# Float64 weights made into fp32 words on the chip: the low word added as an integer

## The chip, the cores and the metric

One core of a Trainium2 chip runs the whole program. The time is device microseconds (us) of one execution. The names of the engines are those of the profile: PE is the matrix engine (TensorE), DVE is VectorE, ACT is ScalarE, POOL is GpSimd, and SP issues transfers.

## What is computed

Linear attention over 32 memory slots, then two MLPs. The weights `w_a`, `w_b`, `w_out` (of both MLPs) come as float64.

```
a = softmax(phi, axis=seq);  k_m = a^T k;  v_m = a^T v          # per batch (4) and head (8), seq 576
attn = softmax(q k_m^T / 8) v_m                                 # -> x: 2304 tokens x 512
x = ((x @ w_a) * (x @ w_b)) @ w_out                             # d_ff 1536
h = x @ w_in;  g = where(h > 0, h, exp(min(h, 0)) - 1)          # d_ff 2048
out = g @ w_out2                                                # 2304 x 512
```

## The kernel before

**Stages.** The attention runs first (L541 to L614), one batch after another: softmax of phi, key and value sums `pk`, scores `sc`, their softmax, and the transposed result `tp_x`, which `split_sb` (L76) splits into a high and a low fp32r part, `xhi` and `xlo`. From the last batch on the first MLP is woven in. `step_u` (L508) multiplies the weights by `v_m` (tile `u_ps`, result split into `u`), `steps_ab` (L616) makes the two products and multiplies them (`a_sb`, split into `gh`, `gl`), and `steps_o1` (L662) makes the product with `w_out` (`o1_ps`, which the profile shows as `o_ps`, evicted into `y`). The second MLP follows with `step_h` (L763, tile `h_ps`) and `steps_o2` (L802). Each product is three fp32r matmuls: high by high, high by low, low by high.

**Order.** Everything from the attention on stands in an order written out by hand, engine by engine. `step` (L253) issues the matmuls of one step on PE, then goes through a string of letters ("0f1a2"): `a` to `d` are the step's evictions, `f` is a share of the weight conversion, the digits are operations deferred by a step or two. Products lie in PSUM tiles `ps` of two banks, at first two of them, from the last batch on four. A matmul group that opens a tile waits until the tile's former content is read.

**Weights.** A unit is a block of weights of 128x512 float64 values; there are 68. A load puts it into one of three `raw` tiles. Then `piece` (L165) takes one slot of the unit at a time, seven slots for a unit. ACT makes `a`, the magnitude of the high word read as fp32 (`magnitude`, L118), and `lw`, the low word as a bf16 number (`low_word`, L126). DVE limits `a` (slot 0, L181), shifts it (slot 1, L184), splits off the low part of the unit before (slot 2, L163), puts the sign in (slot 3, L189), cuts the power of two out of `a` (slot 4, L193), scales `lw` by it (slot 5, L199), and adds (slot 6, L209). A unit of the stage "ab" is then ready as `ush`; others are split once more into a rounded high part (ACT, L154) and a rest (DVE, L163). With `ahead` set, ACT's two operations for the next unit are issued in slots 4 and 5, before the add. `fill(amount)` adds to a credit and runs one slot for each whole point of it; `fill(7)` in the attention runs one unit.

**Buffers.** `a` and `lw` have two tiles each, `a_sb` has three.

Of the kernel before, what the change touches and what calls it, by code (L numbers as in the profile page):

```python
# [7 lines left out]
F32 = mybir.dt.float32  # L8
F32R = mybir.dt.float32r
BF16 = mybir.dt.bfloat16  # L10
U32 = mybir.dt.uint32
U16 = mybir.dt.uint16
I64 = mybir.dt.int64
AF = mybir.ActivationFunctionType
ALU = mybir.AluOpType
AX = mybir.AxisListType
PSUM = bass.MemoryType.PSUM
LARGEST = float(0x1DFFFFF) * 2.0 ** 8


@with_exitstack
def attention_then_two_mlps(ctx, tc, q, kv, kv_left, phi, w_ab, w_o1, w_i2, w_o2, out):
# [13 lines left out]
    nc = tc.nc  # L36
    B, P, KC, S = q.shape
# [8 lines left out]
    HS = S // 2  # L46
# [15 lines left out]
    conv = ctx.enter_context(tc.tile_pool(name="conv", bufs=2, reuse_waits="tile"))  # L62
# [18 lines left out]
    NRAW, NSHORT, NPAIR, NLONG = 3,6,3,4  # L81
    units = []
# [19 lines left out]
    cu = {}  # L102
    seq = []
    ready = {}
    live = {False: 0, True: 0}
    state = {"loaded": 0, "n": 0, "slot": 0, "ahead": False}
# [11 lines left out]
    def magnitude(n):  # L118


        if n < NU and "a" not in cu[n]:
            a = conv.tile([P, 512], U32, tag="a", name="a", bufs=2)
            nc.scalar.activation(out=a.bitcast(F32), in_=cu[n]["h"].bitcast(F32), func=AF.Abs, scale=65536.0)  # L123
            cu[n]["a"] = a

    def low_word(n):  # L126
        if n < NU and "lw" not in cu[n]:
            t = conv.tile([P, 512], BF16, tag="lw", name="lw", bufs=2)
            nc.scalar.activation(out=t, in_=cu[n]["l"], func=AF.Copy, scale=2.0 ** -52)
            cu[n]["lw"] = t  # L130

    def ahead():
# [4 lines left out]
    def whole_words(n):  # L137
        return n < NU and units[n][0][0] == "ab"

    def to_hi(n):  # L140

        if n < 0 or whole_words(n):
            return True
        key, long, _ = units[n]
        if key == own:
            hi, lo = [pb.tile([P, 512], F32R, name=x, bufs=1) for x in ("ulh", "ull")]
        elif live[long] == (NLONG if long else NPAIR):
            return False
        else:
            live[long] += 1  # L150
            tag, nh, nl = ("ul", NLONG, NLONG) if long else ("us", NSHORT, NPAIR)
            hi = conv.tile([P, 512], F32R, tag=tag + "h", name=tag + "h", bufs=nh)
            lo = conv.tile([P, 512], F32R, tag=tag + "l", name=tag + "l", bufs=nl)
        nc.scalar.activation(out=hi, in_=cu[n]["a"].bitcast(F32), func=AF.Copy)  # L154
        ready[key] = hi, lo
        return True
# [8 lines left out]
    def piece():  # L165

        n, slot = state["n"], state["slot"]
        if n > NU:
            return False
        whole = n < NU  # L170
        if whole and slot == 0:
            magnitude(n)
            low_word(n)
        a = cu[n]["a"] if whole else None
        if slot == 1 and not to_hi(n - 1):
            return False
        if slot == 6 and whole_words(n) and live[False] == NSHORT:
            return False
        if whole and slot == 0:

            nc.vector.tensor_scalar(out=a.bitcast(F32), in0=a.bitcast(F32), scalar1=2.0, scalar2=LARGEST,  # L181
                                    op0=ALU.max, op1=ALU.min)
        elif whole and slot == 1:
            nc.vector.tensor_scalar(out=a, in0=a, scalar1=4, scalar2=1,  # L184
                                    op0=ALU.logical_shift_left, op1=ALU.logical_shift_right)
        elif slot == 2:
            to_lo(n - 1)
        elif whole and slot == 3:
            nc.vector.scalar_tensor_tensor(out=a, in0=cu[n]["h"], scalar=0x80000000, in1=a,  # L189
                                           op0=ALU.bitwise_and, op1=ALU.bitwise_or)  # L190
        elif whole and slot == 4:
            p2 = cu[n]["raw"].bitcast(BF16)[:, 0:512]
            nc.vector.tensor_scalar(out=p2.bitcast(U16), in0=a.bitcast(U16).rearrange("p (n w) -> p n w", w=2)[:, :, 1],  # L193
                                    scalar1=0xFF80, scalar2=None, op0=ALU.bitwise_and)
            cu[n]["p2"] = p2
            if state["ahead"]:
                low_word(n + 1)
        elif whole and slot == 5:
            nc.vector.tensor_tensor(out=cu[n]["lw"], in0=cu[n]["lw"], in1=cu[n]["p2"], op=ALU.mult)  # L199
            if ("unit",) not in seq:  # L200
                load_unit()
            if state["ahead"]:
                magnitude(n + 1)
        elif whole and slot == 6:
            to = a.bitcast(F32)
            if whole_words(n):
                live[False] += 1
                to = ready[units[n][0]] = conv.tile([P, 512], F32R, tag="ush", name="ush", bufs=NSHORT).bitcast(F32)
            nc.vector.tensor_tensor(out=to, in0=a.bitcast(F32), in1=cu[n]["lw"], op=ALU.add)  # L209
            if whole_words(n):  # L210
                cu.pop(n)
        slot += 1
        state["n"], state["slot"] = (n + 1, 0) if slot == 7 else (n, slot)
        return True

    def weights(key):
# [11 lines left out]
    credit = [0.0]  # L228

    def fill(amount):  # L230
        credit[0] += amount
        while credit[0] >= 1.0:
            credit[0] -= 1.0
            if not piece():
                credit[0] = 0.0


    RATE_AB, RATE_U, RATE_O1 = 1.0, 1.0, 3.0
    RATE_H, RATE_O2 = 2.5, 3.0
    ORDER, ORDER_H, ORDER_O2 = "0f1a2", "fab0c1df2", "0f1fa2"  # L240

# [38 lines left out]
    pu = es_u.enter_context(tc.tile_pool(name="pu", bufs=2, reuse_waits="tile"))  # L280
    rim = ctx.enter_context(tc.tile_pool(name="rim", bufs=1, side="right", reuse_waits="tile"))
    edge = rim.tile([P, 24], F32, name="edge")
    es_y = ExitStack()
    py = es_y.enter_context(tc.tile_pool(name="py", bufs=1, side="right", reuse_waits="tile"))
    y_all = py.tile([P, KC * NT], F32, name="y")
# [249 lines left out]
    es_b = ExitStack()  # L535
    with tc.manual_schedule():
        nc.gpsimd.memset(edge, 0.0)
        nc.scalar.activation(out=edge, in_=edge, func=AF.Exp)
        make_identity(nc, ident)
        nc.vector.tensor_reduce(out=parity, in_=ident.rearrange("p (s u) -> p u s", u=2), op=ALU.add, axis=AX.X)  # L540
# [24 lines left out]
        for i in range(B):  # L565
# [27 lines left out]
            else:  # L593
                es_l.close()
                es_p.close()
                pb = es_b.enter_context(tc.tile_pool(name="pb", bufs=2, side="right", reuse_waits="tile"))
# [18 lines left out]

        def steps_ab(f, b, amount):  # L616
            u = u_t.pop((f, b))
            a_sb = pb.tile([P, 2, HS], F32, tag="a_sb", name="a_sb", bufs=3)
            flat = a_sb.rearrange("p a s -> p (a s)")
            parts, done = [], 0  # L620
            while done < S:
                t = max(x for x in range(NB) if first[x] <= b * S + done)
                o = b * S + done - first[t]
                if o == 0:
                    if not inner:
                        inner.extend(pb.tile([P, N1], F32R, name=x, bufs=1) for x in ("gh", "gl"))
                    p = 256 * PLACE1[f % G][t]
                    g_t[f, t] = [x[:, p:p + BLOCKS[t]] for x in inner]
                w = min(S - done, BLOCKS[t] - o)
                parts.append((flat[:, done:done + w], *[x[:, o:o + w] for x in g_t[f, t]]))  # L630
                done += w
            for n in range(2):
                ps = pstile("ab_ps")

                def pe():
                    for kk in range(2):
                        for i, (w, x) in enumerate(((0, xhi), (0, xlo), (1, xhi))):
                            for h in range(2):
                                nc.tensor.matmul(  # L639
                                    ps[:, h, 0:HS], u[:, kk, w, n * P:n * P + P], x[b][:, kk, h * HS:(h + 1) * HS],  # L640
                                    start=(kk == 0 and i == 0), stop=(kk == 1 and i == 2),
                                )

                def evac():
                    if n == 0:
                        nc.scalar.activation(out=a_sb, in_=ps[:, :, 0:HS], func=AF.Copy)  # L646
                    else:
                        nc.vector.tensor_tensor(out=a_sb, in0=a_sb, in1=ps[:, :, 0:HS], op=ALU.mult)
                        defer(1, lambda: [nc.scalar.activation(out=gh, in_=a, func=AF.Copy) for a, gh, _ in parts])  # L649
                        defer(2, lambda: [nc.vector.tensor_tensor(out=gl, in0=a, in1=gh.bitcast(F32), op=ALU.subtract)  # L650
                                          for a, gh, gl in parts])

                step(pe, evac, amount)
# [59 lines left out]
        for kind, *args in order:  # L713
# [6 lines left out]
            else:  # L720
# [6 lines left out]
                t = b - 1  # L727
# [128 lines left out]
        for f in range(NF2):  # L856
            for k in range(NPART):
                t = TURN2[f % G][k] if f else k
# [63 lines left out]
```

## Time and profile before

| | us |
|---|---|
| median of 3 runs | 790.51 (789.45 to 790.68) |
| the profiled execution, its own time | 790.06 |
| its span, first to last instruction | 788.3 |
| PE busy in it | 768.9 (98%) |
| PE weight loads (PEld) | 675.4 (86%) |
| DVE busy | 594.8 (75%) |
| ACT busy | 408.9 (52%) |

The span is the time from the first to the last instruction; 1.8 us of the execution lie outside it. The rows further down come from this one execution. Matmuls are pipelined and their ends are modelled, so a stretch in which PE is shown busy can still hold waits; the starts of the matmuls tell it. The granted clock is 1.00 in every stretch up to the last matmul.

### The profile page before, as it was taken

The numbers are of one execution on the slowest core, as the hardware profiler recorded it, in microseconds if no ns is written. First come the engines' busy times: TensorE is split into PE (matmuls) and PEld (weight loads), VectorE is DVE, ScalarE is ACT, GpSimd is POOL, SyncE is SP. The second block draws the span as 40 slices with busy tenths as digits, with TensorE's granted clock in tenths as the row PEclk, the third lists the DMA queues.
The fourth block names the chain that finished last, engine by engine and source line by source line (L and its number), as shares of the span: only waits on it lengthen the run. The fifth ranks groups of instructions, "written<-read, shape, count | busy, mean of one in ns | idle before, by whom it ended". The sixth has DMA issues, their size and how long they took to land.

```text
span 788.3 us, 12416 instructions
## 1 busy us (share of the span) xinstructions
PE 768.9 (98%) x5084; PEld 675.4 (86%) x5084; DVE 594.8 (75%) x977; ACT 408.9 (52%) x684; POOL 38.8 (5%) x83
## 2 busy tenths in 40 slices
PE   4899999999999999999999999999999999999997
PEld 4788889888998999899888888888888888888886
DVE  5799985877877787787997438778877877885564
ACT  4555764534362435253688555556456625762460
POOL 2000000000000000000000000000000000000000
PEclk9999999999999999999999999999999999999999
DMA  9970232111212121122002001101111110100006
GB/s 340 409 281 27 58 104 72 57 61 54 81 29 81 55 81 55 54 68 68 27 5 87 17 1 53 54 28 54 54 36 46 54 54 27 53 1 1 1 1 241
DMA packets 17066, 57.70 MB, mean 73 GB/s; under 512 B 1776, under 2 KB 1776, under 8 KB 17008
## 3 DMA queue, kind: packets, MB, share of 16 engines
q0 software_dynamic: 8784, 31.99, 13.5%
q1 hardware_dynamic: 8224, 24.91, 8.2%
q8 instruction: 40, 0.66, 0.3%
q14 instruction: 18, 0.15, 0.1%
HBM read 52.17 MB, written 4.72 MB: 72 GB/s over the span
## 4 chain that ended last, share of the span: by engine, by line
PE 89%; DVE 5%; ACT 1%; issue 0%; DVEq 0%
PE h_ps L775 25%; PE o_ps L822 25%; PE ab_ps L639 18%; PE o_ps L675 18%; PE u_ps L522 2%; DVE ssm L485 1%; DVE y L490 1%; DVE u L533 0%; DVE y L474 0%; DVE xlo L78 0%; DVE smx L473 0%; DVE a L189 0%; ACT y L683 0%; ACT a L123 0%; PE tp_x L498 0%
## 5 line engine op out<-in xcount | busy, mean ns | idle before, releaser
L639 PE MATMUL ab_ps<-xhi,u 128*128 128x288 f32 x768 | 139.1, 298 | 0.1
L639 PEld LDWEIGHTS ab_ps<-xhi,u 128*128 128x128 f32 x768 | 114.5, 188 | 6.3 <-ACT gh L649 3.7
L822 PE MATMUL o_ps<-ull,g2h 128*128 128x512 f32 x288 | 112.1, 389 | 0.0
L822 PE MATMUL o_ps<-ulh,g2h 128*128 128x512 f32 x288 | 112.0, 389 | 0.0
L775 PE MATMUL h_ps<-yl,ush 128*128 128x512 f32 (+1 forms) x320 | 107.6, 369 | 0.0
L775 PE MATMUL h_ps<-yh,usl 128*128 128x512 f32 (+1 forms) x320 | 107.6, 368 | 0.0
L775 PE MATMUL h_ps<-yh,ush 128*128 128x512 f32 (+1 forms) x320 | 107.2, 367 | 0.0
L822 PE MATMUL o_ps<-ulh,g2l 128*128 128x512 f32 x288 | 100.3, 389 | 0.0
L794 DVE SCALAR_TENSOR_TENSOR e<-e,th 128x512 f32<-128x512 f32 (+1 forms) x64 | 48.3, 755 | 61.5 <-ACT e L791 61.1
L785 ACT ACTIVATE e<-h_ps 128x512 f32<-128x512 f32 (+1 forms) x64 | 41.6, 651 | 91.7 <-PE h_ps L775 85.6
L639 PE MATMUL ab_ps<-xlo,u 128*128 128x288 f32 x384 | 82.1, 295 | 0.0
L675 PE MATMUL o_ps<-gh,ulh 128*128 128x512 f32 (+1 forms) x240 | 72.9, 369 | 1.6 <-ACT y L683 1.6
L646 ACT ACTIVATE a_sb<-ab_ps 128x576 f32<-128x576 f32 x48 | 31.3, 653 | 80.9 <-PE ab_ps L639 80.9
L675 PE MATMUL o_ps<-gl,ulh 128*128 128x512 f32 (+1 forms) x240 | 72.7, 368 | 0.0
L675 PE MATMUL o_ps<-gh,ull 128*128 128x512 f32 (+1 forms) x240 | 72.6, 367 | 0.0
L797 DVE TENSOR_TENSOR g2l<-e,g2h 128x512 fp32r<-128x512 f32 (+1 forms) x64 | 48.4, 756 | 24.9 <-ACT g2h L796 24.5
L775 PEld LDWEIGHTS h_ps<-yh,ush 128*128 128x128 f32 x320 | 59.5, 188 | 8.5
L775 PEld LDWEIGHTS h_ps<-yh,usl 128*128 128x128 f32 x320 | 59.3, 188 | 7.5
L775 PEld LDWEIGHTS h_ps<-yl,ush 128*128 128x128 f32 x320 | 59.2, 188 | 7.3
L834 DVE TENSOR_TENSOR y<-o_ps,y 128x1024 f32<-128x1024 f32 (+1 forms) x44 | 51.0, 1194 | 18.0 <-PE o_ps L822 17.8
L822 PEld LDWEIGHTS o_ps<-ulh,g2l 128*128 128x128 f32 x288 | 54.0, 188 | 11.3
L822 PEld LDWEIGHTS o_ps<-ulh,g2h 128*128 128x128 f32 x288 | 54.1, 188 | 11.2
(95 smaller groups left out, 1273.6 us busy)
## 6 DMA issues: line engine op xcount, KB each, us to landing
raw<-in_w_o_dram POOLq DMA_DIRECT2D x27, 512.0 KB, 3.9
raw<-in_w_ab_dram POOLq DMA_DIRECT2D x18, 512.0 KB, 3.8
kv_t<-in_kv_dram SPq DMA_DIRECT2D x16, 512.0 KB, 9.9
raw<-in_w_i_dram POOLq DMA_DIRECT2D x16, 512.0 KB, 3.8
y<-in_q_dram SPq DMA_DIRECT2D x8, 576.0 KB, 10.3
out_dram<-y SPq DMA_DIRECT2D x8, 512.0 KB, 2.8
raw<-in_w_ab_dram SPq DMA_DIRECT2D x6, 512.0 KB, 9.1
phi_t<-in_phi_dram SPq DMA_DIRECT2D x3, 576.0 KB, 10.0
```

The source lines that it names most:

```text
L485: nc.vector.tensor_reduce(out=sm, in_=at, op=ALU.add, axis=AX.X)
L490: nc.vector.tensor_tensor(out=at, in0=at, in1=sm.to_broadcast(list(at.shape)), op=ALU.mult)
L522: nc.tensor.matmul(ps[j:j + M, o, k * 256:k * 256 + 256], vt[r, 2 * p + o, 2 * k + c], w[r, c * 256:c * 256 + 256], start=True, stop=True, ...
L639: nc.tensor.matmul(ps[:, h, 0:HS], u[:, kk, w, n * P:n * P + P], x[b][:, kk, h * HS:(h + 1) * HS], start=(kk == 0 and i == 0), stop=(kk == ...
L646: nc.scalar.activation(out=a_sb, in_=ps[:, :, 0:HS], func=AF.Copy)
L675: nc.tensor.matmul(ps[:, s], w[:, cc], g[:, s], start=(n == 0 and i == 0), stop=(n == len(fs) - 1 and i == 2),)
L775: nc.tensor.matmul(ps[:, s], w[:, c], x[:, c, s], start=(c == 0 and i == 0), stop=(c == KC - 1 and i == 2),)
L785: nc.scalar.activation(out=e, in_=ps, func=AF.Relu, scale=-1.0)
L794: nc.vector.scalar_tensor_tensor(out=e, in0=e, scalar=1.0, in1=th, op0=ALU.add, op1=ALU.mult)
L797: defer(1, lambda: nc.vector.tensor_tensor(out=gl, in0=e, in1=gh.bitcast(F32), op=ALU.subtract), 1)
L822: nc.tensor.matmul(ps[:, k, :], g[:, c * P:(c + 1) * P], w, start=(f == fs[0] and i == 0), stop=(f == fs[-1] and i == 2),)
L834: nc.vector.tensor_tensor(out=dst, in0=ps[:, 0:n], in1=dst, op=ALU.add)
```

## The change

The arithmetic of a unit is made in another way. ACT now writes `lw` in fp32: the low word times 2^-27 plus an offset of 2^25, which is a [128,1] tile `offset` (a POOL memset at the start). The offset fixes the exponent, so that the rounded low word stands as an integer in the float's bits. DVE shifts `a` left by three bits only, combines the sign with an exclusive or, and adds the bits of `lw` as a 32-bit integer. The slots of L193 and L199 are gone, and a unit has five slots. The built program makes the integer add with one instruction over 1024 16-bit halves in a row of 128 partitions; the order shows it as ISA. `low_word(n + 1)` is now issued behind slot 3 and `magnitude(n + 1)` behind the add; the next unit's load is issued behind slot 3. `fill` multiplies its amount by 5/7, the head's `fill(7)` is so one unit as before, and RATE_U goes from 1.0 to 1.4, which is one slot as before. `a_sb` has two tiles in place of three. The orders on PE and SP are the same as before; POOL has one memset more.

```diff
-LARGEST = float(0x1DFFFFF) * 2.0 ** 8
+LARGEST = float(0x1DFFFFF) * 2.0 ** -11
...
-            nc.scalar.activation(out=a.bitcast(F32), in_=cu[n]["h"].bitcast(F32), func=AF.Abs, scale=65536.0)
+            nc.scalar.activation(out=a.bitcast(F32), in_=cu[n]["h"].bitcast(F32), func=AF.Abs, scale=0.125)
...
-            t = conv.tile([P, 512], BF16, tag="lw", name="lw", bufs=2)
-            nc.scalar.activation(out=t, in_=cu[n]["l"], func=AF.Copy, scale=2.0 ** -52)
+            t = conv.tile([P, 512], U32, tag="lw", name="lw", bufs=2)
+            nc.scalar.activation(out=t.bitcast(F32), in_=cu[n]["l"], func=AF.Identity, scale=2.0 ** -27, bias=offset)
...
-        if slot == 6 and whole_words(n) and live[False] == NSHORT:
+        if slot == 4 and whole_words(n) and live[False] == NSHORT:
             return False
         if whole and slot == 0:
 
-            nc.vector.tensor_scalar(out=a.bitcast(F32), in0=a.bitcast(F32), scalar1=2.0, scalar2=LARGEST,
+            nc.vector.tensor_scalar(out=a.bitcast(F32), in0=a.bitcast(F32), scalar1=2.0 ** -18, scalar2=LARGEST,
                                     op0=ALU.max, op1=ALU.min)
         elif whole and slot == 1:
-            nc.vector.tensor_scalar(out=a, in0=a, scalar1=4, scalar2=1,
-                                    op0=ALU.logical_shift_left, op1=ALU.logical_shift_right)
+            nc.vector.tensor_scalar(out=a, in0=a, scalar1=3, scalar2=None, op0=ALU.logical_shift_left)
         elif slot == 2:
             to_lo(n - 1)
         elif whole and slot == 3:
             nc.vector.scalar_tensor_tensor(out=a, in0=cu[n]["h"], scalar=0x80000000, in1=a,
-                                           op0=ALU.bitwise_and, op1=ALU.bitwise_or)
-        elif whole and slot == 4:
-            p2 = cu[n]["raw"].bitcast(BF16)[:, 0:512]
-            nc.vector.tensor_scalar(out=p2.bitcast(U16), in0=a.bitcast(U16).rearrange("p (n w) -> p n w", w=2)[:, :, 1],
-                                    scalar1=0xFF80, scalar2=None, op0=ALU.bitwise_and)
-            cu[n]["p2"] = p2
-            if state["ahead"]:
-                low_word(n + 1)
-        elif whole and slot == 5:
-            nc.vector.tensor_tensor(out=cu[n]["lw"], in0=cu[n]["lw"], in1=cu[n]["p2"], op=ALU.mult)
+                                           op0=ALU.bitwise_and, op1=ALU.bitwise_xor)
             if ("unit",) not in seq:
                 load_unit()
             if state["ahead"]:
-                magnitude(n + 1)
-        elif whole and slot == 6:
-            to = a.bitcast(F32)
+                low_word(n + 1)
+        elif whole and slot == 4:
+            to = a
             if whole_words(n):
                 live[False] += 1
-                to = ready[units[n][0]] = conv.tile([P, 512], F32R, tag="ush", name="ush", bufs=NSHORT).bitcast(F32)
-            nc.vector.tensor_tensor(out=to, in0=a.bitcast(F32), in1=cu[n]["lw"], op=ALU.add)
+                ready[units[n][0]] = conv.tile([P, 512], F32R, tag="ush", name="ush", bufs=NSHORT).bitcast(F32)
+                to = ready[units[n][0]].bitcast(U32)
+            nc.vector.tensor_tensor(out=to, in0=a, in1=cu[n]["lw"], op=ALU.add)
             if whole_words(n):
                 cu.pop(n)
+            if state["ahead"]:
+                magnitude(n + 1)
         slot += 1
-        state["n"], state["slot"] = (n + 1, 0) if slot == 7 else (n, slot)
+        state["n"], state["slot"] = (n + 1, 0) if slot == 5 else (n, slot)
         return True
...
-        credit[0] += amount
+        credit[0] += amount * 5 / 7
...
-    RATE_AB, RATE_U, RATE_O1 = 1.0, 1.0, 3.0
+    RATE_AB, RATE_U, RATE_O1 = 1.0, 1.4, 3.0
...
+    offset = rim.tile([P, 1], F32, name="offset")
...
+        nc.gpsimd.memset(offset, 2.0 ** 25)
...
-            a_sb = pb.tile([P, 2, HS], F32, tag="a_sb", name="a_sb", bufs=3)
+            a_sb = pb.tile([P, 2, HS], F32, tag="a_sb", name="a_sb", bufs=2)
```

DVE in the attention of the second batch: one unit (L181 to L209, now L181 to L200) between the softmax of phi and that of the scores. Before:

```order
L181 TENSOR_SCALAR a<-a 128x512
L184 TENSOR_SCALAR a<-a 128x512
L189 SCALAR_TENSOR_TENSOR a<-raw,a 128x512
L193 TENSOR_SCALAR raw<-a 128x512
L199 TENSOR_TENSOR lw<-lw,raw 128x512
L209 TENSOR_TENSOR ush<-a,lw 128x512
L362 TENSOR_REDUCE nm<-phi_t 128x1 x2
L473 TENSOR_REDUCE smx<-sc 128x32
```

And now:

```order
L181 TENSOR_SCALAR a<-a 128x512
L184 TENSOR_SCALAR a<-a 128x512
L188 SCALAR_TENSOR_TENSOR a<-raw,a 128x512
L200 ISA ush<-a,lw 128x1024
L356 TENSOR_REDUCE nm<-phi_t 128x1 x2
L467 TENSOR_REDUCE smx<-sc 128x32
```

Two instructions of the six are gone, and nothing else has moved there.

DVE around the first `o1` products (`gl`: rest of `g`; `ull`: rest of a unit; `u`: rest of `u_ps`, which frees that PSUM tile). Just ahead of the first row stands that unit's L193. Before:

```order
L199 TENSOR_TENSOR lw_1175<-lw_1175,raw_608 128x512
L650 TENSOR_TENSOR gl_789<-a_sb_1143,gh_788 128x576
L209 TENSOR_TENSOR a_1191<-a_1191,lw_1175 128x512
L181 TENSOR_SCALAR a_1213<-a_1213 128x512
L184 TENSOR_SCALAR a_1213<-a_1213 128x512
L163 TENSOR_TENSOR ull_1227<-a_1191,ulh_1226 128x512
L189 SCALAR_TENSOR_TENSOR a_1213<-raw_914,a_1213 128x512
L193 TENSOR_SCALAR raw_914<-a_1213 128x512
L199 TENSOR_TENSOR lw_1208<-lw_1208,raw_914 128x512
L209 TENSOR_TENSOR ush_1248<-a_1213,lw_1208 128x512
L181 TENSOR_SCALAR a_1246<-a_1246 128x512
L533 TENSOR_TENSOR u_1250<-u_ps_1251,u_1250 128x4x256
```

And now:

```order
L200 ISA a_1181<-a_1181,lw_1166 128x1024
L645 TENSOR_TENSOR gl_783<-a_sb_1133,gh_782 128x576
L181 TENSOR_SCALAR a_1200<-a_1200 128x512
L184 TENSOR_SCALAR a_1200<-a_1200 128x512
L163 TENSOR_TENSOR ull_1213<-a_1181,ulh_1212 128x512
L188 SCALAR_TENSOR_TENSOR a_1200<-raw_904,a_1200 128x512
L200 ISA ush_1230<-a_1200,lw_1197 128x1024
L181 TENSOR_SCALAR a_1232<-a_1232 128x512
L527 TENSOR_TENSOR u_1234<-u_ps_1235,u_1234 128x4x256
```

The add of the first unit stands ahead of `gl` instead of behind it, and L193 and L199 of both units are gone ahead of the instruction that frees the PSUM tile.

ACT at the same place, from the two `u` evictions on. Before:

```order
L531 ACTIVATE u_1270<-u_ps_1271 128x4x256
L683 ACTIVATE y_77<-o1_ps_1291 128x512
L683 ACTIVATE y_77<-o1_ps_1301 128x512
L129 ACTIVATE lw_1310<-raw_1189 128x512
L123 ACTIVATE a_1315<-raw_1189 128x512
```

And now:

```order
L525 ACTIVATE u_1254<-u_ps_1255 128x4x256
L678 ACTIVATE y_78<-o1_ps_1275 128x512
L129 ACTIVATE lw_1286<-raw_1164,offset_74 128x512
L678 ACTIVATE y_78<-o1_ps_1289 128x512
L123 ACTIVATE a_1299<-raw_1164 128x512
```

A low word now stands between the evictions of the first two `o1` tiles. The PSUM tiles are dealt out otherwise, too: the third `o1` tile of this group took over the tile that the first eviction freed, and now takes the one that the rest of `u` (L533, now L527) frees.

## Rows read from the trace of the kernel before

**Rows 1.** Busy time by stretch: us, then PE, PEld, DVE, ACT, POOL; clock; DMA.

```profile
76.00:105.00 29.00, 27.43 (x244) 23.26 (x243) 27.27 (x51) 22.43 (x37) 2.23 (x4) 1.00 0.25 74
105.00:783.70 678.70, 678.70 (x4036) 598.04 (x4034) 506.51 (x807) 345.44 (x561) 31.32 (x56) 1.00 0.16 50
```

**Rows 2.** Chain of work that ended last: start, us, what.

```profile
130.01 9.59 PE ab_ps L639 x72
...
759.23 24.49 PE o_ps L822 x108
```

**Rows 3.** Groups of instructions by line and shape: busy us, mean ns, idle before.

```profile
L129 ACT ACTIVATE lw<-raw 128x512 bf16<-128x512 uint32 x68 | 44.9, 661 | 14.0 <-DVE ush L209 14.0
...
L199 DVE TENSOR_TENSOR lw<-lw,raw 128x512 bf16<-128x512 bf16 x68 | 28.7, 421 | 1.2
...
L479 ACT ACTIVATE y<-y 128x1024 f32<-128x1024 f32 x4 | 4.2, 1062 | 0.3 <-DVE y L474 0.3
...
L396 ACT ACTIVATE a_left<-tl_a,parity 128x128 f32<-128x128 f32 x8 | 2.5, 367 | 0.0
...
L438 ACT ACTIVATE vt<-pt 128x128 f32<-128x128 f32 x4 | 1.1, 283 | 0.0
```

**Rows 4.** Timeline, DVE, second batch: start us, us, instruction, idle before.

```profile
34.51 0.43 DVE L193 TENSOR_SCALAR raw<-a 128x512 uint16<-128x512 uint16 x1
...
35.43 0.69 DVE L209 TENSOR_TENSOR ush<-a,lw 128x512 f32<-128x512 f32 x1
...
41.15 1.22 DVE L78 TENSOR_TENSOR xlo<-tp_x,xhi 128x1024 fp32r<-128x1024 f32 x1
```

**Rows 5.** Timeline, PE, where the third batch's scores begin.

```profile
41.76 0.27 PE L388 MATMUL tl_a<-ident,rest 128*128 128x128 f32 x1
42.48 3.81 PE L447 MATMUL sc<-y 128*128 128x128 f32 x32 [0.45 <-issue]
```

**Rows 6.** Timeline, PE, the first ab product.

```profile
58.24 0.42 PE L639 MATMUL ab_ps<-xlo,u 128*128 128x288 f32 x2
58.74 0.80 PE L639 MATMUL ab_ps<-xhi,u 128*128 128x288 f32 x4
```

**Rows 7.** Timeline, DVE, softmax sums of the third batch.

```profile
53.88 1.53 DVE L485 TENSOR_REDUCE ssm<-y 128x32 f32<-128x1024 f32 x2
```

**Rows 8.** Timeline, ACT, the exponentials ahead of them.

```profile
52.49 1.36 ACT L479 ACTIVATE y<-y 128x1024 f32<-128x1024 f32 x2
```

**Rows 9.** Timeline, DVE, the second ab product.

```profile
67.71 0.75 DVE L648 TENSOR_TENSOR a_sb<-a_sb,ab_ps 128x576 f32<-128x576 f32 x1
```

**Rows 10.** Timeline, PE, that product and the last transposes.

```profile
66.78 0.42 PE L639 MATMUL ab_ps<-xhi,u 128*128 128x288 f32 x2
...
74.54 0.43 PE L639 MATMUL ab_ps<-xhi,u 128*128 128x288 f32 x2
75.41 1.06 PE L498 MATMUL tp_x<-ident,y 128*128 128x128 f32 x8 [0.43 <-DVE y L490]
```

**Rows 11.** Timeline, DVE, at the first o1 products.

```profile
95.59 0.43 DVE L193 TENSOR_SCALAR raw<-a 128x512 uint16<-128x512 uint16 x1
...
101.65 1.22 DVE L533 TENSOR_TENSOR u<-u_ps,u 128x1024 fp32r<-128x1024 f32 x1
```

**Rows 12.** Timeline, ACT, at the first o1 products.

```profile
97.78 0.63 ACT L154 ACTIVATE ulh<-a 128x512 fp32r<-128x512 f32 x1 [0.37 <-DVE a L209]
...
100.35 1.93 ACT L531 ACTIVATE u<-u_ps 128x1024 fp32r<-128x1024 f32 x2
```

**Rows 13.** Timeline, PE, the third o1 tile of the second group.

```profile
100.86 0.39 PE L675 MATMUL o_ps<-gh,ull 128*128 128x512 f32 x1
102.81 0.50 PE L675 MATMUL o_ps<-gh,ulh 128*128 128x512 f32 x1 [1.56 <-ACT y L683]
```

**Rows 14.** Waits: engine, line, waited for: us, times, longest.

```profile
DVE a L181 <- ACT a L123: 9.5, 8, 2.4
```

**Rows 15.** Windows of line L181 alone: DVE busy us and count.

```profile
76.00:105.00 29.00, 2.11 (x5) 1.00 0.25 74
```

## The prediction

> **What bounds the kernel now.** I read the busy time by stretch first, then the chain, then the timelines of the places where PE stands. From 105 us to 783.7 us PE is busy all of the time at full granted clock [rows 1], and in the chain its matmuls follow one another at 24.49/108 = 0.227 us for 512 columns and 9.59/72 = 0.133 us for 288 [rows 2]; so nothing waits in these 679 us. DVE has 506.5 of these 678.7 us to do, ACT 345.4 [rows 1]. A cheaper unit on DVE is worth nothing there. Up to 32 us the start waits for transfers that the change leaves alone. What DVE can give back lies between 32 and 105 us, in four waits of PE: 0.45 us before the third batch's scores [rows 5]; 58.74 - (58.24 + 0.27) = 0.23 us in the first ab product, a pair of whose matmuls takes 0.27 us otherwise [rows 2, 6]; 75.41 - (74.54 + 0.27) = 0.60 us before the last transposes [rows 10]; 102.81 - (100.86 + 0.23) = 1.72 us before the third o1 tile of the second group [rows 13]. Together 3.0 us: no more can be won.
>
> **The unit on DVE.** L193 and L199 leave. From the start of L193 to the start of the add it is 35.43 - 34.51 = 0.92 us [rows 4]; so much earlier the add can start. Its own price is not in the trace. It has 1024 halves for each partition. The nearest rows are a two-tensor instruction over 512 bf16 elements at 0.421 us, the old fp32 add over 512 at 0.69, and one over 1024 fp32 elements at 1.22 [rows 3, 4, 11]. At the rate of bf16 elements 1024 halves cost what 512 fp32 elements do, 0.69; at the rate of fp32 elements 1.22. I take 0.69, since halves are 16 bits wide as in the bf16 row, which is the row of its kind; 1.22 is the upper bound. [...]
>
> The trace shows the 16-bit row at 0.421 us beside 0.69 for as many fp32 elements [rows 3, 4]. [...]
>
> **The low word on ACT.** Same shape, fp32 out, and a [128,1] operand as bias, where there was an immediate. The trace has 0.661 us for the old form; for 128x128 an activation with a [128,1] operand takes 0.367 us and one without 0.283 [rows 3]. So the price of the operand is 0 to 0.09 us; I take 0.09. Over 68 units it is 6 us of an engine that has 22.4 of 29 us to do in its fullest stretch [rows 1], and counts only where ACT stands in the path, below.
>
> **Place 1, 42 us.** PE's score matmuls wait for the PSUM tile that L78 reads, from 41.15 to 42.37 [rows 4]; PE itself is ready at 41.76 + 0.27 = 42.03 [rows 5]. The unit at 34.51 is in front of L78 on DVE, and so L78 ends at 42.37 - 0.92 = 41.45. Next late is PE itself, the wait is gone: 0.45 us.
>
> **Place 2, 58 us.** DVE's chain to the rest of `u` goes through one more unit (0.92 us) and then through L485 at 53.88 [rows 7]. L485 needs the exponentials, the larger of which ends at 52.49 + 1.06 = 53.55 [rows 3, 8] and follows PE, now 0.45 us earlier: 53.1. So the chain moves by 0.78 us, PE by 0.45, and 0.33 is more than the 0.23 us of the wait: all of it goes.
>
> **Place 3, 75 us.** DVE's product starts at 67.71, and right ahead of it stands L193; it leaves, L189 goes behind the product, and the shorter L184 comes in its place. The product then starts when its matmuls are done, at 66.78 + 0.42 = 67.20 and a semaphore later, 0.45 us earlier instead of 0.51 [rows 9, 10]. From it the path goes over `gh`, a low word and `u` on ACT, then to the softmax that PE waits for. The low word costs its 0.09. Won: 0.36 of 0.60 us. What is late next is the same softmax.
>
> **Place 4, 101 us.** Today `ulh` waits on ACT for DVE's add, 0.37 us, and starts at 97.78 [rows 12]. The new add starts at 95.59 [rows 11] and ends at 96.28; `ulh` is then held by ACT alone, which is free at 97.78 - 0.37 = 97.41, and 97.43 with the dearer low word ahead: 0.35 us won. A second low word before the evictions of `u` takes back 0.09, so these start at 100.09 instead of 100.35 [rows 12]. The rest of `u` on DVE needs the first of the two, 1.93/2 = 0.97 us, and starts at 101.1 instead of 101.65 [rows 11]; it ends 1.2 us later, at 102.3. By the order the third o1 tile now waits for this instruction, and PE goes on at 102.3 instead of 102.81 [rows 13]: 0.49 us won. On ACT a low word now stands between the evictions of the first two tiles, and the fourth tile takes over what the second eviction frees. The evictions of `u` end at 100.09 + 1.93 = 102.02; two evictions of 0.63, as long as `ulh` for the same 512 columns [rows 12], and a low word of 0.75 end at 104.0, or some 0.2 sooner since neighbours on ACT overlap; PE comes there at 102.3 + 6 x 0.23 = 103.7. I take 0.1 us off: 0.39 won. Without PE's six matmuls as a cover the low word's 0.75 us would be the price.
>
> **What costs nothing.** Two tiles of `a_sb` instead of three: ACT's copy of a product waits for the rest `gl` of the one before last. If DVE is late, the copy is late, but PE writes four PSUM tiles in turn and comes back to this one three groups of 12 x 0.133 = 1.6 us later [rows 2]; the price up to 4.8 us of lateness is nothing. The load issued two slots earlier comes to a POOL queue that does nothing else; its memset at the start delays nothing that PE waits for, as the first matmuls wait for the transfers. The 5/7 keeps the units' pace.
>
> **Sum.** 0.45 + 0.23 + 0.36 + 0.39 = 1.43 us off the profiled execution's own 790.06 (span 788.3): **788.6 us**. The median of the three runs, 790.51, lies 0.45 above that execution, and the fastest 0.6 below; the change's worth is of the size of this scatter. About 0.2%, 1.6 us, is what a measurement of this kernel can tell from no change.
>
> **Rivals.** (1) The add takes 1.22 us. A unit gains 0.92 - 0.53 = 0.39. Place 1 gives 0.40 (L78 ends at 41.98, before 42.03, less the semaphore), place 2 nothing (both chains move by 0.4), place 3 its 0.36, since the add lies behind it, place 4 about 0.2 (the second add on the way to 101.65 is dear too). Together 1.0: 789.1. For it speaks that no row shows the instruction.
> (2) Place 4 stays as it is, since ACT, not DVE, was named at 102.81 [rows 13], and the reorder takes the gain: 790.06 - 1.04 = 789.0. Against it speaks the 0.37 us for which ACT itself waited for DVE [rows 12].
> (3) More than I count goes, since one late operation shifts all that follow: up to the 3.0 us, 787.0; a middle of 787.7.
> (4) Slower: DVE now waits for ACT's magnitude at the start of each unit. It used to be issued before the add, which covered it; now it is issued behind the add, and L181 follows at once. Today this wait is 9.5 us, 8 times [rows 14]. Between 76 and 105 us DVE has 29.0 - 27.27 = 1.73 us of idle time and 5 units [rows 1, 15]. Each gains 0.92 and would lose a wait w. From w = 0.92 + 1.73/5 = 1.27 us on PE is late by 5 (w - 0.92) - 1.73. With w = 2, an activation plus an eviction ahead of it, that is 3.7 us; less places 1 to 3 (1.04), the time is 790.06 + 2.6 = 792.7. Against it: ACT has 6.6 us of idle time in the stretch, and before the units at 76 to 105 us the credit comes in single slots, so that the magnitude has a step's time.
>
> **How the numbers follow.** The forecast, 1.1 to 1.9 us won, has a chance of 0.48; rival 3 0.17; rivals 1 and 2 together 0.25; rival 4 0.10. A gain over 1.6 us takes rival 3 and half of the forecast: faster 0.41. Rival 4 is over 0.2% slower in 8 of its 10: slower 0.08. Within 0.2%: 0.51. The range leaves out the outer part of rival 3, below 787.0, and rival 4: 787.0 to 790.4, the upper end being both rivals 1 and 2 (789.4) and the scatter of the runs above the profiled one.
>
> **What would show it.** In the new profile: the add's mean at 0.69 or 1.22 us; the low word at 0.66 or 0.75; PE's idle time before the third batch's scores gone; the rest of `u` ahead of 58 us no longer named; before the transposes 0.2 us instead of 0.43; before the third o1 tile about 1.2 instead of 1.72 us and named by DVE's L527; DVE's sum of busy time lower by 68 x (0.43 + 0.42) = 58 us with PE's unchanged. The prediction is wrong if PE shows a wait after 105 us, or if the transfers of the first 32 us move.

## The result, and the profile after

The changed kernel takes 798.73 us (median of 4 runs, 798.33 to 799.21) where the kernel before takes 789.98 on the same chip (788.78 to 790.68): a ratio of 1.0113, 95% interval 1.0095 to 1.013. It is slower by 8.75 us; the forecast was 788.6.

Busy time by stretch, in the layout of [rows 1]. The chain of waits names nothing but PE from 101.30 us to the end of its last matmul, 792.42, and the stretch from 105 us to there answers to the second of [rows 1].

```profile
76.00:105.00 29.00, 27.97 (x246) 23.74 (x245) 25.05 (x44) 23.09 (x39) 2.64 (x5) 1.00 0.29 79
105.00:792.42 687.42, 687.40 (x4028) 596.33 (x4026) 460.18 (x685) 349.92 (x559) 30.00 (x55) 1.00 0.16 49
```

DVE has lost its work as intended: 460 us of it after 105 us in place of 506.5. PE is busy without a gap at full granted clock, as before, and yet it needs longer: over the whole execution it is busy for 778.7 us in place of 768.9. The chain (start, us, what) shows which matmuls, beside [rows 2]:

```profile
128.50 9.58 PE ab_ps L634 x72
...
149.74 16.80 PE o_ps L670 x72
...
767.20 25.22 PE o_ps L817 x108
```

The products `ab_ps` of 288 columns follow one another as before (9.58 against 9.59 us for 72). The last o2 product, 512 columns wide, takes 25.22/108 = 0.2335 us apiece where it took 24.49/108 = 0.2268. So 6.7 ns are lost on a matmul, with nothing waiting, in a stretch where no weight is being converted any more (DVE's last add of a unit starts at 718.71 us). The groups by line and shape (busy us, mean ns) say the same, 394 or 395 ns in place of 389 or 390 in each of the six groups of 512 columns of o2 and h, and show what became of the unit (L200, which the order shows as ISA, stands here as CUSTOM_DVE_ANT_0); beside [rows 3]:

```profile
L817 PE MATMUL o_ps<-ulh,g2h 128*128 128x512 f32 x288 | 113.8, 395 | 0.0
...
L200 DVE CUSTOM_DVE_ANT_0 a<-a,lw 128x1024 uint16<-128x1024 uint16 x44 | 30.3, 688 | 0.8
...
L129 ACT ACTIVATE lw<-raw,offset 128x512 f32<-128x512 uint32 x68 | 51.2, 753 | 6.0 <-DVE ush L200 6.0
```

The four places of PE, in its timeline (start, us, instruction, idle before), beside [rows 5, 6, 10, 13]:

```profile
41.82 0.27 PE L382 MATMUL tl_a<-ident,rest 128*128 128x128 f32 x1
41.93 1.28 PE L441 MATMUL sc<-y 128*128 128x128 f32 x10
...
57.44 0.42 PE L634 MATMUL ab_ps<-xlo,u 128*128 128x288 f32 x2
57.91 0.79 PE L634 MATMUL ab_ps<-xhi,u 128*128 128x288 f32 x4
...
74.28 1.07 PE L492 MATMUL tp_x<-ident,y 128*128 128x128 f32 x8 [0.30 <-DVE y L484]
...
99.87 0.40 PE L670 MATMUL o_ps<-gh,ull 128*128 128x512 f32 x1
101.30 0.50 PE L670 MATMUL o_ps<-gh,ulh 128*128 128x512 f32 x1 [1.03 <-DVE u L527]
```

The third o1 tile starts at 101.30 in place of 102.81: 1.51 us won, about what was forecast. From there to the end of the span it takes 797.0 - 101.3 = 695.7 us in place of 788.3 - 102.81 = 685.5: **10.2 us lost**. The question for the runs is what makes a matmul of 512 columns slower.

One thing about PE's operands did change, which is in no trace. The allocation of the two programs (bytes within a partition) shows that the new tile `offset`, one column wide, takes 32 bytes at the top of the right side and moves every tile below it:

```
tile, side                              before            after
y            (right)                    192384            192352
gh, gl       (right, moving in o1)      141696, 164224    141664, 164192
yh2, yh3     (right, moving in h)       122752, 139136    122720, 139104
g2h, g2l     (right, stationary in o2)  155520, 173952    155488, 173920
first ush    (left, stationary in h)    34944             36992
first ulh    (left, o1 and o2)          47232             49280
yh1          (left, moving in h)        94336             96384
```

The right side moves by 32 bytes, the left side by 2048, since the two `lw` are now fp32.

### The profile page after: what moved, and what is told of

Read it like the earlier page. It is cut to its first block, busy times and chain, and to the rows that moved or that the text cites. A ratio compares the mean times of both kernels' runs of the same rounds, so it can differ in the third digit from the quotient of the medians.

```text
span 797.0 us, 12293 instructions
## 1 busy us (share of the span) xinstructions
PE 778.7 (98%) x5084; PEld 674.6 (85%) x5084; DVE 543.1 (68%) x841; ACT 414.9 (52%) x684; POOL 37.9 (5%) x84
## 4 chain that ended last, share of the span: by engine, by line
PE 90%; DMA 5%; DVE 3%; ACT 1%; issue 0%; SPq 0%; DVEq 0%
PE o_ps L817 25%; PE h_ps L770 25%; PE ab_ps L634 19%; PE o_ps L670 18%; PE u_ps L516 2%; DMA raw<-in_w_ab_dram 2%; DMA kv_t<-in_kv_dram 1%; DMA phi_t<-in_phi_dram 1%; DVE ssm L479 1%; DVE y L484 0%; DVE u L527 0%; ACT y L678 0%; ACT lw L129 0%; ACT u L525 0%; PE tp_x L492 0%
## 5 line engine op out<-in xcount | busy, mean ns | idle before, releaser
L817 PE MATMUL o_ps<-ulh,g2h 128*128 128x512 f32 x288 | 113.8, 395 | 0.0
L817 PE MATMUL o_ps<-ull,g2h 128*128 128x512 f32 x288 | 113.8, 395 | 0.0
L817 PE MATMUL o_ps<-ulh,g2l 128*128 128x512 f32 x288 | 102.0, 395 | 0.0
L643 DVE TENSOR_TENSOR a_sb<-a_sb,ab_ps 128x576 f32<-128x576 f32 x48 | 36.0, 752 | 50.7 <-PE ab_ps L634 50.4
## 6 DMA issues: line engine op xcount, KB each, us to landing
kv_t<-in_kv_dram SPq DMA_DIRECT2D x16, 512.0 KB, 10.2
phi_t<-in_phi_dram SPq DMA_DIRECT2D x3, 576.0 KB, 10.2
```

The lines of the kernel that those rows point to most:

```text
L817: nc.tensor.matmul(ps[:, k, :], g[:, c * P:(c + 1) * P], w, start=(f == fs[0] and i == 0), stop=(f == fs[-1] and i == 2),)
```

## The experiments

**Which part of the change.** Theory A: the 32 bytes do it. Theory B: the 2048 bytes of the left side. Theory C: the new instructions on DVE and ACT disturb PE.

*The column in the tile `edge`.* On the changed kernel:

```
-    offset = rim.tile([P, 1], F32, name="offset")
+    offset = edge[:, 23:24]
```

> The changed kernel with the bias column kept in the last column of the tile edge, so that no tile of its own is made and every tile on the right side of SBUF lies where it lay before the change; all instructions of the change stay, and the left side's tiles stay 2048 bytes further on. Theory A (the 32 bytes by which the new tile moves the right side's tiles make the matmuls of 512 columns slower): they go back to 0.2268 us apiece, and the time is about 798.7 - 10.2 = 788.5 us. Theory B (the 2048 bytes by which the larger lw moves the left side's tiles do it) and theory C (the new instructions on VectorE and ScalarE disturb TensorE): 0.233 us apiece, 798.7 us as with the change whole.

787.84 us (787.35 to 789.27), ratio to before 0.998, interval 0.997 to 0.9989. All of the loss is gone, and what is left is a small gain. The chain of this run:

```profile
129.37 9.59 PE ab_ps L634 x72
...
150.63 16.34 PE o_ps L670 x72
...
388.88 22.05 PE h_ps L770 x108
440.85 13.85 PE h_ps L770 x72
...
758.42 24.49 PE o_ps L817 x108
```

The last product is back at 24.49 us, to the hundredth what it was [rows 2], with every instruction of the change in place. Theories B and C fall.

*The tile alone.* On the kernel before:

```
     edge = rim.tile([P, 24], F32, name="edge")
+    offset = rim.tile([P, 1], F32, name="offset")
...
+        nc.gpsimd.memset(offset, 2.0 ** 25)
```

> The kernel before with nothing but the new tile of one column and its fill on GpSimd, which moves every tile on the right side of SBUF by 32 bytes; no instruction of the conversion is changed. Theory A: 1872 matmuls at 0.2333 in place of 0.2268 us, about 790 + 10 to 12 = 800 to 802 us. Theories B and C: 790 us.

800.29 us, ratio 1.0137 (1.0122 to 1.0152). A tile that nothing reads costs 10.65 us:

```profile
768.61 25.22 PE o_ps L824 x108
```

*The left side alone, with two `a_sb`.* On the kernel before:

```
-            t = conv.tile([P, 512], BF16, tag="lw", name="lw", bufs=2)
+            t = conv.tile([P, 1024], BF16, tag="lw", name="lw", bufs=2)[:, 0:512]
...
-            a_sb = pb.tile([P, 2, HS], F32, tag="a_sb", name="a_sb", bufs=3)
+            a_sb = pb.tile([P, 2, HS], F32, tag="a_sb", name="a_sb", bufs=2)
```

> The kernel before with the two lw tiles twice as large (their second halves unused), which moves the left side's tiles by 2048 bytes as the change does, and with two a_sb tiles to make room; the right side stays. Theory B: about 800 us, 0.233 us for a matmul of 512 columns. Theories A and C: 790 us, 0.2268 us.

789.9 us, ratio 1.0002 (0.9993 to 1.0012). Neither the 2048 bytes nor the third `a_sb` tile matter.

*A tile of 64 bytes.* On the changed kernel:

```
-    offset = rim.tile([P, 1], F32, name="offset")
+    offset = rim.tile([P, 16], F32, name="offset")
```

> The changed kernel with the new tile 16 columns wide, so that the right side's tiles move by 64 bytes in place of 32 and lie on multiples of 64 again. Theory A, if it is the place within 64 bytes that counts: 788.5 us. If it is any other address than before's, or a larger multiple that counts (theory A2): slow still, about 798.7. Theories B and C: 798.7 us.

796.08 us, ratio 1.0079 (1.0062 to 1.0096). Theory A stands, but not in its form with 64 bytes: multiples of 64 are still slow, though less so. In this trace the matmuls of o1, and of h in its third and fourth part of the tokens, are as slow as in the changed kernel; those of o2 follow one another at 0.2307 us on average.

**Place or distance.** h goes over four parts of the tokens, the first of 768, the others of 512. In the changed kernel the matmuls of its second part, whose operands both lie on the left (`ush` and `yh1`), were hardly slower, 0.2302 us, and the few of o1 with both on the right 0.227 to 0.230. So it is either the place of each operand (theory P) or the distance between the two operands of one matmul (theory R).

*A tile of 128 bytes.* As above, with `[P, 32]`.

> The changed kernel with the new tile 32 columns wide, so that the right side's tiles move by 128 bytes and lie on multiples of 128, as before the change (64 of them were not enough). Two theories are left of what a matmul of 512 columns wants: theory P (place: each of its two operands on a multiple of 128 bytes) and theory R (relation: the distance between the moving and the stationary operand, modulo 128 bytes or more; in the changed kernel one of the two lies on the left and one on the right nearly always, and the few matmuls with both on the right took 227 to 230 ns in place of 233). Theory P, and theory R modulo 128: 788 us, 0.227 us apiece. Theory R modulo 256 or more: slow, 795 to 799 us.

797.39 us, ratio 1.0095 (1.008 to 1.0111). All operands lie on multiples of 128 bytes, as before the change, and the loss is there:

```profile
765.81 25.22 PE o_ps L817 x108
```

*The left side by 32 bytes.* On the kernel before, the right side in its place:

```
+    shim = ctx.enter_context(tc.tile_pool(name="shim", bufs=1, reuse_waits="tile"))
+    gap = shim.tile([P, 8], F32, name="gap")
     conv = ctx.enter_context(tc.tile_pool(name="conv", bufs=2, reuse_waits="tile"))
```

> The kernel before with a tile of 32 bytes at the foot of the left side and nothing else: the left side's tiles move by 32 bytes, the right side stays. Both theories: about 800 us, 0.233 us for the matmuls with one operand on each side. They part on the matmuls with both operands on the left (ab_ps of 288 columns, h_ps of the second part with 512). Theory P: these become slower too, 0.229 to about 0.234 us for h_ps of the second part. Theory R: these stay as they were, 0.229 and 0.133 to 0.135 us.

799.99 us, ratio 1.0128 (1.0111 to 1.0145):

```profile
353.19 9.60 PE ab_ps L642 x72
...
769.28 25.22 PE o_ps L825 x108
```

The `ab_ps`, both of whose operands were moved together, stay at 9.60 us for 72, and h of the second part at 0.2302 us, as in the changed kernel. Those that lose 6 ns and more are the pairs that were moved against one another.

*Both sides, 128 bytes apart in all.* The changed kernel with a gap of `[P, 24]` at the foot of the left side.

> The changed kernel with 96 bytes more at the foot of the left side: with the right side 32 bytes lower and the left side 96 bytes higher, the distance between them has changed by 128 bytes, while neither side lies on multiples of 64. Theory R modulo 128: 788 us, 0.227 us. Theory R modulo 256 or more: slow, as f1. Theory P: 798 us or more, 0.233 us or more.

797.62 us, ratio 1.0099 (1.0084 to 1.0114), and the last product again takes 25.22 us. The tile of 128 bytes had the same distance between the sides with other places, and the two times agree within 0.3 us.

*Both sides, 2048 bytes apart in all.* The kernel with the tile alone (800.29 us), a gap of `[P, 504]` on the left and two `a_sb`.

> The kernel before with the new tile (right side 32 bytes lower), 2016 bytes more at the foot of the left side and two a_sb tiles to make room: the distance between the sides has changed by 2048 bytes, and neither lies on multiples of 64. Theory R: 790 us, 0.227 us for a matmul of 512 columns, whether the modulus is 128 or up to 2048. Theory P: 800 us or more.

789.38 us, ratio 0.9998 (0.9989 to 1.0008):

```profile
758.52 24.49 PE o_ps L827 x108
```

No operand on the right lies on a multiple of 64, and nothing is lost. Theory P falls; it is the distance.

**The modulus.** *A tile of 256 bytes.* On the changed kernel, `[P, 64]`.

> The changed kernel with the new tile 64 columns wide, so that the right side's tiles move by 256 bytes. In the kernel before, the moving and the stationary operand of nearly every matmul of 512 columns lie 256 bytes apart modulo 512; here they come to 0 modulo 512, where in every kernel so far only h_ps of the second part lies (0.2295 us on average, some matmuls 231 or 236 ns). Theory R modulo 256 (256 and 0 are the same): 788 us, 0.227 us. Theory R modulo 512, with 0 as h_ps of the second part shows it: some 1700 matmuls at 1 to 3 ns more, 790 to 793 us. If 256 modulo 512 is the only distance without loss: 795 to 798 us.

788.15 us, ratio 0.9978 (0.9969 to 0.9988):

```profile
757.36 24.49 PE o_ps L817 x108
```

128 bytes are slow (797.39 us), 256 are free (788.15): in these runs the distance counts modulo 256.

*The second part of h by 256 bytes.* On the kernel with the column in `edge`:

```
+            if blk == 1:
+                space = pool.tile([P, 64], F32, tag="space", name="space", bufs=1)
```

> The changed kernel with the bias column in the tile edge (right side as before), and a tile of 256 bytes ahead of yh1 and yl1 on the left, which brings the moving operand of h_ps's second part from 0 to 256 bytes modulo 512 away from its weights; all else as in the run with the column in edge alone (787.8 us). Theory R modulo 512: its 192 matmuls go from 0.2295 to 0.2267 us, 0.5 us less, 787.3 us. Theory R modulo 256, with another cause for the 0.2295: 787.8 us, and 0.2295 stays.

787.84 us, ratio 0.9977 (0.9967 to 0.9986), the very median of the run without the move. The 0.2295 us of these matmuls (0.2292 with the steps between groups) did not go. The records show where they come from, in the kernel before as here: twelve of the part's sixteen groups of 12 matmuls come right behind matmuls of 384 columns (h's first part), and there the first nine take 224 to 236 ns and the last three 226 or 227, 230.1 on average; the other four groups come behind o2's 512 columns and take 226.7 ns like everything else. So it is the step from one shape to the other, and not the distance; why the step costs this is not shown.

*The second part of h by 32 bytes.* The same with `[P, 8]`, so that one part's tiles `yh1` and `yl1`, on the left like their weights, go out of step.

> The changed kernel with the bias column in the tile edge (787.84 us), and a tile of 32 bytes ahead of yh1 and yl1: on the left side alone, the moving operand of h_ps's second part lies 32 bytes modulo 256 away from its weights in place of 0. If the distance modulo 256 decides for any pair of tiles: its 192 matmuls go from 0.2293 to 0.2333 us and no others change, 0.8 us more, 788.6 us. If it takes one operand on either side: nothing changes, 787.8 us.

789.46 us, ratio 0.9996 (0.9986 to 1.0005). In the chain, beside that of the run with the column in `edge`:

```profile
387.56 22.20 PE h_ps L773 x108
439.69 13.92 PE h_ps L773 x72
...
758.47 24.49 PE o_ps L820 x108
```

The h products grow (22.05 to 22.20, 13.85 to 13.92) and o2 stays. The matmuls of this part went to 0.2332 us, as theory R has it. The cost is larger than expected: 1.6 us by the medians of the two runs, 1.39 if each is taken against the kernel before in its own runs (789.87 and 789.64), and (758.47 - 387.56) - (758.42 - 388.88) = 1.37 us by the rows, not 0.8: the third and fourth part of h became 1.2 ns a matmul slower with it. That lies in the twelve of their 32 groups that come right behind the second part's: 229.7 ns a matmul, where the other twenty keep their 226.7. So the matmuls out of step also slow the first ones of the group behind them: 192 x 4.1 ns in the part itself and 144 x 3.1 ns behind it make 0.8 + 0.4 us, and four groups of 18 in o2, behind the same part, have the last 0.1.

The means of the start-to-start time of 512-column matmuls, from the records of all kernels, by the distance of the moving operand from the stationary one:

```
distance modulo 256   o2      o1      h, parts 3 and 4   h, part 2
0                     226.9   227.2   226.7              229.5 ns
32                    233.3   -       -                  233.2
64                    230.7   -       -                  -
128                   232.9   232.4   232.9              -
192                   -       233.3   233.4              -
224                   -       233.3   233.3              -
```

**What the gain comes from.** *The clamp three times.* On the kernel with the column in `edge`, the instruction at the head of a unit is repeated, which gives DVE back what the change took off it:

```
+            for _ in range(3):
                 nc.vector.tensor_scalar(out=a.bitcast(F32), in0=a.bitcast(F32), scalar1=2.0 ** -18, ...
```

> The changed kernel with the bias column in the tile edge (787.84 us), and the clamp at the head of each unit done three times over, with the same outcome: 2 x 0.42 = 0.84 us more of VectorE per unit, about what the change took away (0.424 + 0.421), while everything else of the change stays. Theory U (what the change wins is the shorter unit on VectorE, in the waits of TensorE before 105 us): the gain of 1.8 us goes again but for a few tenths, about 789.3 us, and the wait of the third o1 tile comes back from 1.2 to about 1.7 us. Theory V (it comes from something else of the change, such as the load that is issued earlier or the a_sb tiles): 787.8 us. In both the 68 units after the first 105 us cost nothing, 0.227 us for a matmul of 512 columns.

790.7 us, ratio 1.0008 (0.9999 to 1.0017) to 789.87 for before in the same runs. The gain is gone, and it goes where theory U has it: from the start of the transpose `tl_a` ahead of the third batch's scores to the third o1 tile, PE takes 61.41 us, with the column in `edge` alone 59.47, and in the kernel before 102.81 - 41.76 = 61.05. So V, by which 787.8 was to stay, falls. But the run lost 1.4 us more than expected, and so it does not show to the last tenth that the shorter unit is all of the gain. PE's waits (us in total, times, longest):

```profile
PE o_ps L671 <- ACT y L679: 1.1, 1, 1.1
...
PE o_ps L671 <- DVE ull L163: 0.6, 1, 0.6
PE sc L442 <- ACT y L474: 0.5, 1, 0.5
PE ab_ps L635 <- DVE u L528: 0.5, 1, 0.5
```

The long instructions sit in one slot, and other waits came up than the one I named. The third o1 tile's stays at 103.27 - (101.75 + 0.23) = 1.29 us, now named by ACT's L679, and does not go back to 1.7. Beside it the third batch's scores (L442) wait again, o1 waits for `ull` ahead of 100.24 us, and `ab_ps` waits ahead of 341.71 us, in the stretch where I had said that a unit costs nothing. So with 1.34 us in one slot DVE's units are no longer quite free after 105 us.

## Why the prediction was wrong

**The step that failed is the first.** "From 105 us to 783.7 us PE is busy ... so nothing waits in these 679 us" is true of both kernels. What I made of it, that these matmuls keep their 0.227 us, is not: those of 512 columns went to 0.233. The term that I had wrong stands under **What costs nothing**: I costed the tile `offset` by its memset alone, not by the 32 bytes that it takes, and put it at nothing. Alone in the kernel before it costs 10.65 us. Nearly every o1 matmul has its weights on the left and its moving operand on the right, and so have the third and fourth part of h; o2 has them the other way round. All lay at a multiple of 256 bytes from each other, and came to 32 or 224 modulo 256.

By the records of the changed kernel: 864 matmuls of o2 by 6.4 ns, 384 of h by 6.6 and some 396 of o1 by 6.1 make 5.6 + 2.5 + 2.4 = 10.5 us. Small changes in the other shapes (384 and 288 columns, some 0.5 us faster together, and 0.1 slower in h's second part) leave 10.1 to 10.2, which is what was lost behind 101.30 us.

None of my rivals had this in it, rival 4 looked for the loss in a wait, and the two signs by which I said the prediction would be wrong (a wait of PE after 105 us, moved transfers) did not show. One sign of the list before them did: PE's busy time, to be unchanged, rose by 9.8 us. (DVE's fell by 52 us, 594.8 to 543.1, where 58 were said.)

A reading under **What costs nothing** is not what the profile names, at no cost: "the first matmuls wait for the transfers". The waits of the kernel before name POOL's `pair` L551 for the first transposes (5.3 us; in some of the other runs ACT's `phi_t`), and the memset stands ahead of it. The transposes start at 5.29 us before and 5.28 now.

**The other steps held**, in sum and mostly one by one:

- The add takes 0.688 us (0.69 taken; rival 1's 1.22 is out), the low word 0.753 (0.75 taken). The two rows of the low word give 753 - 661 = 92 ns more than the old form [rows 3], between two forms that also differ in their output type.
- Place 1: the wait is gone, the scores start at 41.93 in place of 42.48: 0.55 us won (0.45 said), since they follow 0.11 us behind the transpose and not 0.27.
- Place 2: PE came 0.80 us earlier and not 0.45, so the wait stayed, 0.47 us between the pairs against 0.50. By here 58.74 - 57.91 = 0.83 us were won, 0.68 were said.
- Place 3: 75.41 - 74.28 = 1.13 us by here, 1.04 said; 0.30 us of the wait are left, where 0.2 were said. The 0.06 us taken for a semaphore were an estimate: the product starts at 66.49, 0.11 us behind the shown end of its last matmuls, 65.96 + 0.42 = 66.38.
- Place 4: 1.51 us by here, 1.53 said. The wait is 101.30 - (99.87 + 0.23) = 1.20 us and named by DVE's L527, both as written. The overlap of neighbours on ACT that I counted with is there: the two `u` evictions of the kernel before take 1.93 us together [rows 12] and 1.01 each, 0.1 less than one behind the other. Rival 2 is out.
- Rival 4: DVE's wait for the magnitude has grown, to 12.5 us, 9 times, from 9.5 us, 8 times [rows 14], but PE shows no lateness from it: DVE is down to 25.05 us between 76 and 105.

The places are less sure one by one than their sum. From the start of `tl_a` to the third o1 tile PE takes 61.05 to 61.10 us in the five kernels with the old arithmetic, and 59.43 to 59.64 in the eight with the new one and a single clamp: 1.4 to 1.7 us, as forecast. But in two of the old ones (the left side moved by 2048 and by 32 bytes) the third batch's scores follow `tl_a` without a wait, at 41.74 and 42.22 us, and the time goes in ahead of 105 us all the same; and with the column in `edge` the wait of place 2 is gone, as I had said (58.90 - 58.63 = 0.27). So it was luck which of the places showed the gain in one execution. `tl_a` itself starts anywhere from 40.65 to 42.74 us, which is more than the gain.

With the tile out of the way the change does what the sum said: 787.84 us against 789.64 for before in those runs, 1.8 us less, where 1.43 were forecast. This version is 0.2% faster (0.1 to 0.3) than the kernel before.

## What to carry to other kernels

A new tile can move its neighbours, as the one column here did, by 32 bytes, and those cost 10.65 us; before costing it at nothing, compare the addresses of what the bounding engine reads before and after, and put a small constant into the unused end of a tile that is there already (787.84 us here). Where PE never waits, look in the next profile at its time per matmul first (0.227 to 0.233 us here), not at its waits. One run with the new tile alone in the old kernel tells such a cost from that of the work.

## What the runs showed of the hardware

A matmul of 128x128 by 512 columns in fp32r, in a stream where each loads its own weights (o2: 864 loads for 864 matmuls), took 0.227 us when its moving and its stationary operand lay a multiple of 256 bytes apart within the partition, and 0.231 to 0.234 us at the other distances that came up (32, 64, 128, 192 and 224 bytes modulo 256); the place of either alone did not matter (797.4 and 797.6 us at the same distance with other places; 789.4 us with neither side on a multiple of 64). The other shapes showed it less: `ab_ps` of 288 columns, half of whose matmuls are 128 bytes out of step in all kernels, took 131.2 ns at 0 and 134.8 at 128 on average in the kernel before; o1 of 384 columns, over all of its matmuls, took 173.4 there, 173.8 in the changed kernel (224), 175.9 with the tile of 128 bytes (128) and 176.4 with that of 64 (192). What ran just ahead counts too, and either way: in the run with 64 bytes nine groups of `ab_ps`, whose own operands had not moved against one another, took 130 ns a matmul in place of 133. Why it is 256 bytes, and what in PE takes the longer time, no run tells. Other distances than these six were not tried.
